# Sliding-window attention on one core: two half-empty key blocks as 32-query products, shared edge columns, a new order

## The chip, the cores and the metric

The kernel runs on one core of one Trainium2 chip. The metric is the device time of one execution in microseconds (us), the median of several runs. The engines of the core are TensorE (PE; its weight loads are listed as PEld), VectorE (DVE), ScalarE (ACT), GpSimd (POOL) and SyncE (SP), which issues most transfers. Each works through its own list of instructions in order and waits on semaphores for the others.

## What is computed

Four residual layers over a sequence of 2,048 positions with 512 features, in bf16: linear attention (A), sliding-window attention (B), A, B. Both have 32 heads of 16 features. The change lies in B:

```python
def _B_ref(x, wqkv, wo):
    B, S, D = x.shape
    H = 32; Dh = D // H; W = 256
    ...
    scores = jnp.einsum("bhqd,bhkd->bhqk", q, k) * (Dh ** -0.5)
    idx = jnp.arange(S)
    mask = (idx[:, None] - idx[None, :] >= 0) & (idx[:, None] - idx[None, :] < W)
    scores = jnp.where(mask[None, None], scores, -1e9)
    p = _softmax(scores, axis=-1)
    o = jnp.einsum("bhqk,bhkd->bhqd", p, v)
    return (lambda x, *d: x.transpose(*d))(o, 0, 2, 1, 3).reshape(B, S, D) @ wo

x = A_x
x = x + _A_ref(_layernorm(x, axis=-1), A_wqkv, A_wo)
x = x + _B_ref(_layernorm(x, axis=-1), B_wqkv, B_wo)
x = x + _A_ref(_layernorm(x, axis=-1), A_wqkv, A_wo)
x = x + _B_ref(_layernorm(x, axis=-1), B_wqkv, B_wo)
```

So a query sees itself and the 255 keys before it.

## The kernel before

**Stages.** `build` (L252) makes a graph of operations in this order: the keys of the first layer A (`layer_a_keys`), a `barrier` in which its sums over all positions are closed, `middle(2)`, a second `barrier`, and `middle(3)`. `middle(2)`, here phase 2, runs tile by tile over 16 tiles of 128 positions: the output of the first A, the first B, and already the keys and values of the second A. `middle(3)`, here phase 3, does the output of the second A, the second B and the stores. The queries of the second A stand between.

**Scores.** For a tile j of 128 keys, two blocks b of 64 keys are taken apart. Keys of two heads are interleaved on the 128 partitions (64 keys x 2 heads), so 16 head pairs are worked on (f = 0 to 3, gq = 0 to 3). `b_scores` (L617) multiplies each block with the 256 queries from its own first position on: eight products (L634) in 32x128 array tiles, into four PSUM banks; two exponentials on ScalarE (L644) write them as bf16 into a buffer P (`pb`, for every fourth tile of phase 3 a part of `vp`); a product with a triangle on DVE (L652) zeroes the first 64 columns above the diagonal. A key still reaches up to 255 positions on, so columns 256 to 319 of the block are made by `b_far` (L708): 32 products of 64 columns (L723), two exponentials (L732), and a mask (`far_masks`, L695) for each of the two blocks, either by GpSimd (L703) or by DVE (L704). In P, a block has 384 columns, of which the last 64 (and, for the next tile, the 64 ahead of the first) are zeros.

**Values.** `b_values` (L738) is called twice for each query tile j, for h = 0 and 1, with eight head pairs each. It sums over six key blocks; the part of P for the 128 queries is the stationary operand, the values with a column of ones (34 columns for two heads) the moving one (L753). Of the six blocks, block 2j-4 is the far end of the window, of which only the first 64 queries of the tile see anything; block 2j+1 is the second half of the tile's own keys, which only the last 64 queries see. For the other 64 queries both hold zeros. Then follow the reciprocal of the ones' column (L765) and a product (L766), a transpose by DMA, the output product (L400) and the residual sum (L568), and in phase 2 the normalisation (L361 to L365, two of its steps, L363 and L364, on GpSimd) and keys and values of the next A.

**Order.** `place` (L92) decodes the table at the end of the file: the place of every operation in one global order, the engine of each operation that may run on more than one (PSUM copies on ScalarE or DVE, far masks on DVE or GpSimd, stores issued by SP or GpSimd), and the PSUM bank of each tile. `synchronise` (L133) puts in the waits. The costs in the code (`mm`, `act`, `dve`, `par`) play no part once the table stands.

**Modes.** Three shapes of the array occur: full, 32x128 (scores; `spread`, L550), and 128x32 (denominators of A, `den`, L537: four tiles of 32 columns beside each other).

`b_edge` (L660) is there but not called: `PACK` (L218) is empty.

## Time and profile before

| what | us |
| --- | --- |
| median of 3 runs (416.87 to 417.95) | 416.91 |
| the profiled execution | 415.97 |
| its span, first to last instruction | 414.2 |
| PE busy, of the span | 387.9 (94%) |
| DVE busy | 346.8 (84%) |
| ACT busy | 345.8 (83%) |
| POOL busy | 117.7 (28%) |
| L644, exponentials of the scores, 224 into `pb` | 206.7 |
| L644, 32 into `vp` | 26.5 |
| L753, value products into `ps` from `pb`, 2,560 | 83.2 |
| L732, exponentials of the far scores into `pb`, 50 | 49.6 |
| L703, far masks on POOL, 26 into `pb` | 29.8 |

The chain that ended last, as the page sums it up, is made up of PE 48%, ACT 35%, DVE 9%, DMA 5%. The granted TensorE clock was 0.999 over the span. A busy share is an average: the last fourteen us hold little work on any engine, and the stages before are limited by different engines, so the stretches of the windows have to be read one by one. A line such as L400, L414 or L389 belongs to a helper (products of a tile with a weight, PSUM copies) that many operations share; the names of the tiles tell them apart. Durations of TensorE's products contain the time until the result stands, so starts, not durations, tell how closely products follow each other.

### The profile page before, as it was taken

What the parts mean: (1) busy time and instruction counts of PE and PEld (TensorE: products, weight loads), DVE (VectorE), ACT (ScalarE), POOL (GpSimd) and SP (SyncE); (2) the same over time, 40 slices, a digit from 0 to 9 for tenths busy, and PEclk for the clock granted to TensorE, in tenths of its full rate; (3) what the DMA queues carried; (4) which work ended last, traced back from release to release, by engine and by line L of the source; (5) the groups of instructions that cost most, each with busy time, mean ns of one, the idle gap of its engine ahead of it and who ended that gap; (6) DMA issues with size and microseconds to landing.
All of it is one profiled execution on the core that took longest, in us unless ns stands there. A gap on an engine that the chain in (4) does not pass through costs nothing.

```text
span 414.2 us, 17130 instructions
## 1 busy us (share of the span) xinstructions
PE 387.9 (94%) x7481; PEld 258.5 (62%) x7555; DVE 346.8 (84%) x803; ACT 345.8 (83%) x432; POOL 117.7 (28%) x211
## 2 busy tenths in 40 slices
PE   7999999999999999999999999999999989988886
PEld 3545676766575577565666777586757745556554
DVE  5997898989989988778978689989799687776575
ACT  2624449998999999999997245999999999999992
POOL 4784833111241243230112302220132215230111
PEclk9999999999999999999999999999999999999999
DMA  7545316632233624444213100353306623273361
GB/s 246 177 79 148 104 40 119 131 92 68 64 96 78 110 73 113 80 107 106 56 29 69 26 2 27 93 148 79 81 7 134 137 56 95 60 159 96 93 121 54
DMA packets 67555, 37.83 MB, mean 91 GB/s; under 512 B 48248, under 2 KB 62584, under 8 KB 67480
## 3 DMA queue, kind: packets, MB, share of 16 engines
q1 hardware_dynamic: 67040, 35.54, 36.7%
q8 instruction: 60, 0.98, 1.0%
q0 software_dynamic: 432, 1.18, 0.9%
q14 instruction: 15, 0.12, 0.1%
q10 hardware_dynamic: 8, 0.00, 0.0%
HBM read 6.29 MB, written 2.10 MB: 20 GB/s over the span
## 4 chain that ended last, share of the span: by engine, by line
PE 48%; ACT 35%; DVE 9%; DMA 5%; issue 2%; SPq 1%
ACT pb L644 22%; PE ps L400 17%; PE ps L414 13%; PE ps L753 7%; ACT pb L732 6%; ACT vp L644 5%; PE ps L634 5%; PE ps L475 2%; DMA XQ<-xn 2%; DVE stats L361 2%; DMA xres<-in_A_x_dram 2%; DVE xres L568 1%; DVE XQ L557 1%; PE ps L723 1%; ACT vp L732 1%
## 5 line engine op out<-in xcount | busy, mean ns | idle before, releaser
L644 ACT ACTIVATE pb<-ps 128x1024 bf16<-128x1024 f32 (+2 forms) x224 | 206.7, 1042 | 4.5 <-PE ps L634 3.7
L753 PEld LDWEIGHTS ps<-vB,pb 128*128 128x128 bf16 x2560 | 77.5, 96 | 11.7 <-issue 4.6
L753 PE MATMUL ps<-vB,pb 128*128 128x34 bf16 x2560 | 83.2, 177 | 1.1 <-ACT pb L644 0.6
L414 PE MATMUL ps<-xT,wBp 128*128 128x128 bf16 x1024 | 69.2, 219 | 1.2 <-DVE vp L586 0.5
L414 PEld LDWEIGHTS ps<-xT,wBp 128*128 128x128 bf16 x1024 | 59.2, 98 | 13.6 <-issue 4.4
L423 ACT ACTIVATE tE<-ps 128x512 bf16<-128x512 f32 x64 | 38.5, 612 | 34.3 <-PE ps L400 15.5
L363 POOL TENSOR_SCALAR ve<-mv 128x1 f32<-128x1 f32 x64 | 16.7, 261 | 172.6 <-DVE mv L362 170.5
L634 PE MATMUL ps<-XQ,kB 32*128 32x256 bf16 (+2 forms) x1024 | 49.6, 267 | 5.0 <-ACT vp L644 1.4
L732 ACT ACTIVATE pb<-ps 128x1024 bf16<-128x1024 f32 x50 | 49.6, 1066 | 0.4 <-PE ps L723 0.2
L568 DVE TENSOR_TENSOR xres<-ps,xres 128x512 bf16<-128x512 f32 x63 | 43.1, 685 | 7.6 <-PE ps L400 7.0
L400 PE MATMUL ps<-wA,XQ 128*128 128x512 bf16 x176 | 46.2, 379 | 2.7 <-issue 0.6
L652 DVE TENSOR_TENSOR pb<-pb,tri 128x512 bf16<-128x512 bf16 x112 | 44.7, 412 | 4.0 <-ACT pb L644 3.7
L703 POOL TENSOR_SCALAR_AFFINE_SELECT pb<-pb 128x1024 bf16<-128x1024 bf16 x26 | 29.8, 1148 | 62.9 <-DVE pb L652 32.6
L361 DVE BATCH_NORM_STATS2 stats<-xres 128x6 f32<-128x512 bf16 x64 | 43.6, 686 | 2.6 <-DMA xres<-in_A_x_dram 1.8
L364 POOL TENSOR_TENSOR rs<-ve,negh 128x1 f32<-128x1 f32 x64 | 37.8, 591 | 5.3
L634 PEld LDWEIGHTS ps<-XQ,kB 32*128 32x128 bf16 x1024 | 15.5, 92 | 33.6 <-ACT pb L644 9.2
L414 PE MATMUL ps<-XQ,wA 128*128 128x128 bf16 x512 | 34.7, 219 | 0.3 <-DVE o L766 0.3
L414 PEld LDWEIGHTS ps<-XQ,wA 128*128 128x128 bf16 x512 | 30.4, 98 | 5.7 <-DVE o L766 0.6
L400 PE MATMUL ps<-wBv,xT 128*128 128x512 bf16 x112 | 31.5, 380 | 2.2 <-issue 1.3
L400 PE MATMUL ps<-wBo,oT 128*128 128x512 bf16 x105 | 28.8, 380 | 4.2 <-issue 1.1
L400 PE MATMUL ps<-M,XQ 128*128 128x512 bf16 x112 | 30.7, 380 | 2.1 <-issue 1.0
L765 DVE RECIPROCAL rc<-ps 128x16 f32<-128x16 f32 x64 | 16.1, 252 | 19.3 <-PE ps L753 19.0
(110 smaller groups left out, 532.8 us busy)
## 6 DMA issues: line engine op xcount, KB each, us to landing
vB<-vS SPq DMA_DIRECT2D x64, 136.0 KB, 2.6
kB<-vp SPq DMA_DIRECT2D x64, 128.0 KB, 2.7
wA<-in_A_wqkv_dram SPq DMA_DIRECT2D x3, 512.0 KB, 4.6
out_dram<-xres POOLq DMA_DIRECT2D x9, 128.0 KB, 2.8
xres<-in_A_x_dram SPq DMA_DIRECT2D x2, 512.0 KB, 4.3
pb<-in_B_wqkv_dram SPq DMA_DIRECT2D x1, 1024.0 KB, 5.6
xres<-in_A_x_dram SPq DMA_DIRECT2D x3, 256.0 KB, 4.8
out_dram<-xres SPq DMA_DIRECT2D x6, 128.0 KB, 2.4
```

Source lines behind the costliest of these rows:

```text
L361: self.on("DVE", "stats", lambda e: e.bn_stats(K.stats[:, t, :], K.xres[:, t, :]), key, dve(512), rd=[("xres", t)], wr=[("stats", t)])
L364: self.pow = self.on("POOL", "pow", lambda e: e.tensor_tensor(K.rs[:, t, :], K.ve[:, t, :], K.negh[:], ALU.pow), key + 0.03, (640, 690), r ...
L400: m = e.matmul(K.ps(ps), lhs(c), rhs(c), start=c == 0, stop=c == 3)
L414: m = e.matmul(K.ps(ps)[:, f * P:(f + 1) * P], w(c, f), xT(c), start=c == 0, stop=c == 3)
L423: self.on("ACT", "E", lambda e: e.activation(K.tE[:, s, :], K.ps(ps), ACT.Exp, bias=0.0), key, act(512), wr=[("tE", s)], ps=[ps])
L568: self.on("DVE", "res", lambda e: e.tensor_tensor(K.xres[:, t, :], K.ps(po), K.xres[:, t, :], ALU.add), key, dve(512), rd=[("xres", t)], w ...
L634: m = e.matmul(K.ps(ps[gq])[:, ns * i:ns * i + ns], K.kB[rows, j % 4, 2 * f + b, :, :], K.XQ[rows, f, q:q + ns], start=True, stop=True, ti ...
L644: return e.activation(out(2 * h, 2, ns), i, ACT.Exp, bias=0.0, scale=0.25)
L652: return e.tensor_tensor(x, x, K.tri[:, 0, sh:64].unsqueeze(1).unsqueeze(1).to_broadcast([P, 4, n, 64 - sh]), ALU.mult)
L703: return e.affine_select(out=x, in_=x, compare_op=ALU.is_ge, fill=0.0, base=-2, pattern=[[0, 16], [-2, 64]], channel_multiplier=1)
L732: return e.activation(far(h), i, ACT.Exp, bias=0.0, scale=0.25)
L753: m = e.matmul(K.ps(ps)[:, 34 * u:34 * u + 34], K.P((b // 2) % rp)[:, gq, f, o:o + P], K.vB[:, (b // 2) % 4, b % 2, r, :], start=i == 0, s ...
```

## The change

In `b_values`, for the tiles listed in a new table `HALF` (phase 2: tiles 2 to 15; phase 3: tiles 2 to 8), the two half-empty blocks are taken out of the sum. A new operation `ph`, one for each h, adds them to the same PSUM bank afterwards: for each of the eight head pairs four products of 32 queries and 34 columns, in the array's 128x32 tiles; two take the far block's first 64 queries, two the own second block's last 64. The reads (and so the waits) of both operations are listed block by block.

`PACK` now names tile 9 of phase 3. There the scores of `b_scores` start 32 queries later, and `b_edge` makes columns 0 to 31 and 288 to 319 of each block in one go in place of `b_far`: keys 0 to 31 of a block against the first, keys 32 to 63 against the last, as products of 32 columns in 32x64 array tiles. One DVE product (`ma`) masks the first columns and copies them to their place.

The table of orders, engines and banks is another one. Beside what follows from the above it puts seven PSUM copies of phase 2 from ScalarE to DVE and one from DVE to ScalarE (three small ones around the barriers change sides too), eleven far masks from DVE to GpSimd, and two stores from GpSimd to SP.

```diff
-PACK = {}
+PACK = {3: [9]}
+HALF = {2: tuple(range(2, 16)), 3: tuple(range(2, 9))}
...
     def b_edge(self, j, key):
...
-                        c = 128 * f + 64 * b
-                        m = e.matmul(K.ps(ps[gq])[:, c:c + 64], K.kB[rows, j % 4, 2 * f + b, :, :], bass_view(K.XQ[rows, f, q:q + 32], [[288, 2], [1, 32]]), start=True, stop=True, tile_position=(32 * gq, 0))
+                        c = 64 * f + 32 * b
+                        for u in range(2):
+                            q = P * j + 64 * b + 288 * u
+                            half = slice(64 * u, 64 * u + 64)
+                            m = e.matmul(K.PS[half, ps[gq].banks[0], c:c + 32], K.kB[rows, j % 4, 2 * f + b, 32 * u:32 * u + 32, :], K.XQ[rows, f, q:q + 32], start=True, stop=True, tile_position=(32 * gq, 64 * u))
...
-            self.on("DVE", "gc", lambda e, side=side: e.tensor_copy(side(0), side(32)), key, dve(512), ps=two)
...
-                return e.activation(edge(h), K.pair(two, [[128, 4], [64, 2], [1, 32]]), ACT.Exp, bias=0.0, scale=0.25)
+                return e.activation(edge(h), K.pair(two, [[64, 4], [32, 2], [1, 32]]), ACT.Exp, bias=0.0, scale=0.25)
...
     def b_values(self, j, h, key):
...
-        blocks = [(2 * j, 0), (2 * j + 1, -64), (2 * j - 1, 64), (2 * j - 2, 128), (2 * j - 3, 192), (2 * j - 4, 256)]
+        blocks = [(2 * j, 0), (2 * j - 1, 64), (2 * j - 2, 128), (2 * j - 3, 192)]
+        ends = [(2 * j - 4, 256), (2 * j + 1, -64)]
+        apart = j in self.halves
+        if not apart:
+            blocks += ends
...
-                        m = e.matmul(K.ps(ps)[:, 34 * u:34 * u + 34], K.P((b // 2) % rp)[:, gq, f, o:o + P], K.vB[:, (b // 2) % 4, b % 2, r, :], start=i == 0, stop=i == len(blocks) - 1)
+                        m = e.matmul(K.ps(ps)[:, 34 * u:34 * u + 34], at(b, c, gq, f, P), val(b, 4 * f + gq), start=i == 0 and (not apart or u == 0), stop=not apart and i == len(blocks) - 1, skip_group_check=apart)
...
+        if apart:
+            def put(e):
+                m = None
+                for u in range(8):
+                    f, gq = 2 * h + u // 4, u % 4
+                    for g in range(4):
+                        b, c = ends[g // 2]
+                        m = e.matmul(K.ps(ps)[32 * g:32 * g + 32, 34 * u:34 * u + 34], at(b, c + 32 * g, gq, f, 32), val(b, 4 * f + gq), start=False, stop=True, tile_position=(0, 32 * g), skip_group_check=True)
+                return m
+            self.pe("ph", put, key + 0.01, 32, 34, mode=(128, 32), rd=reads((2 * h, 2 * h + 1), ends), ps=[ps])
```

## The prediction

> **What bounds the kernel now.** I read the windows first, cut at the places where the chain of waits changes its engine. Columns are the stretch, its length, and the busy time of TensorE (PE), weight loads, VectorE (DVE), ScalarE (ACT) and GpSimd (POOL).

> ```profile
> 115.00:170.00 55.00, 52.96 (x1176) 36.63 (x1191) 48.35 (x117) 54.88 (x64) 16.07 (x28) 1.00 0.45 92
> 170.00:205.00 35.00, 33.40 (x688) 21.21 (x683) 29.92 (x68) 34.22 (x41) 8.08 (x13) 1.00 0.35 87
> 205.00:278.00 73.00, 71.00 (x1236) 49.49 (x1249) 62.24 (x142) 52.26 (x77) 15.16 (x28) 1.00 0.23 56
> 278.00:322.00 44.00, 42.69 (x948) 29.66 (x953) 38.64 (x88) 43.28 (x51) 9.30 (x15) 1.00 0.35 79
> 322.00:400.00 78.00, 69.28 (x1667) 45.87 (x1675) 56.38 (x128) 77.29 (x86) 18.50 (x25) 1.00 0.44 100
> ```

> Phase 2 (first sliding-window layer, about 60 to 230 us) uses TensorE and ScalarE up together: 52.96 and 54.88 of 55 us. From 205 to 278 ScalarE has air (52.26 of 73) and TensorE none (71.00). From 278 to 400 it is ScalarE (120.6 of 122 us), with 8.7 us of air on TensorE after 322.

> Then the chain of waits, start and length in us; it names the engine that sets the time in each stretch:

> ```profile
> 161.13 9.20 ACT pb L644 x10
> 170.38 2.33 PE ps L400 x10
> ...
> 252.28 1.79 PE ps L414 x32
> ...
> 379.99 14.24 ACT pb L644 x16
> ```

> So TensorE work taken out of phase 2 is worth its length, ScalarE work taken out of phase 3 (second sliding-window layer, from about 260) too, and TensorE work taken out of phase 3 next to nothing.

> **What TensorE pays now.** Timeline of TensorE; a group's length is from its first start to the modelled end of its last product.

> ```profile
> 44.78 0.24 PE L537 MATMUL ps<-ones,eps 128*32 128x128 bf16 x4
> 44.85 0.40 PE L537 MATMUL ps<-XQ,zs 128*32 128x128 bf16 x16
> 45.18 0.62 PE L414 MATMUL ps<-XQ,wA 128*128 128x128 bf16 x8
> ...
> 86.64 0.41 PE L723 MATMUL ps<-XQ,kB 32*128 32x64 bf16 x32
> ...
> 187.95 0.40 PE L634 MATMUL ps<-XQ,kB 32*128 32x256 bf16 x8
> 188.28 1.37 PE L753 MATMUL ps<-vB,pb 128*128 128x34 bf16 x48
> 189.58 0.40 PE L634 MATMUL ps<-XQ,kB 32*128 32x256 bf16 x8
> ```

> A value product of 34 columns lasts 177 ns alone, so 48 of them start (1370-177)/47 = 25.4 ns apart; call it 25. The far scores, 32 products of 64 columns in four row tiles (188 ns alone), start (410-188)/31 = 7.2 ns apart, 29 ns for four. The denominators are the one operation in the new shape, 128x32: 16 products of 128 columns (219 ns alone) start (400-219)/15 = 12 ns apart on average, their groups of four 56 ns apart, as far as full products of 128 columns do.
> A change of array mode costs too. The last of the 48 value products starts at 188.28+1.37-0.177 = 189.47, the scores at 189.58: 110 ns instead of 25. The last denominator starts at 45.03, the next full product at 45.18: 150 ns instead of 56. About 85 to 95 ns for each change.

> **The change, part by part.**
> *Half blocks (phase 2, tiles 2 to 15; phase 3, tiles 2 to 8; two halves each, so 28 and 14 places).* Each place loses 2 blocks x 8 head pairs = 16 full products: 16 x 25 = 400 ns. It gains 32 products in 8 groups of four, and one stay in another mode. No row shows a group of four column tiles with 34 columns. Bounds: 25 ns a group (nothing in the trace starts its full products closer, and four at once at that pace would be free); 56 ns (the denominators, same shape, longer stream). I take 29, the far scores' group: four small products that do run side by side, nearest in columns. Between a last value product and the scores behind it, 7 x 29 + 110 = 313 ns come in for 400 out: 87 ns saved a place. With 25 it is 115 saved, with 56 and 150 at the exit it is 142 lost.
> [...]
> The order of both built programs counts the mode changes: 152 to 184 in phase 2, 157 to 172 in phase 3. The 28 places explain 28 of the 32 new ones; 4 more cost 4 x 95 ns = 0.4 us. Phase 2: 28 x 87 ns - 0.4 = **2.0 us** off TensorE (2.8 at 25 ns a group; 4.4 more at 56). It lies on the path from 170 to 278; up to 170, where the chain runs through ScalarE, it counts because the next item relieves ScalarE too. In phase 3 the 14 places save some 1.2 us, under the exponentials: 0 on the path. If they cost instead (2 us at 56 ns), the 8.7 us of air after 322 covers part.

> *Copies and masks moved.* In phase 2, ScalarE loses seven PSUM copies (three value, two next-layer value, one query, one transpose) and gains one: mean of such a copy 0.6 to 0.7 us, 0.49 in the chain, so 2.9 to 4 us, more than the 2.0 that TensorE loses. They land on DVE at 0.69 us. DVE gives back 11 far masks, 7 of them in phase 2 (L704, 682 ns, 7.5 us in all), to POOL, where one lasts 1,148 ns (L703). POOL has the time: 16.07 of 55 us busy. Cost 0, covered by POOL's idle time. Without cover, a mask that is late holds POOL's next eps and power (L363, L364: 261 + 591 ns), so the normalisation behind it, and the half blocks that read it.

> *One tile of shared edges (phase 3, tile 9).* Two exponentials of 1,024 columns (1,066 ns, L732) become two of 512 (594 ns, L644): 2 x 472 = 944 ns; the chain's pitch of an exponential, 9.20/10 = 920 ns, scaled by the columns gives 2 x 430. I take **0.9 us**, on the path (322 to 400). The 64 small score products replace 32: 230 ns become 230 (eight at once) to 460 ns, in TensorE's air. The added DVE product is one like L704 (0.69 us), DVE is busy 56 of 78 us there: 0.

> *Waits.* Full blocks no longer wait for the masks of the two end blocks; the new half-block step does, and behind it on TensorE stand scores in 20 of 42 places, which feed ScalarE. Value products (L753) waited for POOL's masks 0.3 us in all, so I take 0 for both. Summed with the prices above, the new order puts every score group of phases 2 and 3 as deep in TensorE's work as the old one, less the saving, to within 0.7 us: no stage is rebuilt.

> Sum: 2.0 + 0.9 = 2.9 us. The profiled execution took 415.97 us (span 414.2), so it would take 413.1; it lies 0.9 under the median of 416.91, from which I count: **414.0 us**.

> **Rivals.**
> A. *The TensorE time turns into waits.* For: up to 170 the chain is ScalarE's. Against: the same phase loses ScalarE copies. Only the edge's 0.9 us is left: 416.0, within 0.3% (1.25 us, about what a measurement of this kernel tells from no change).
> B. *A group of four is paced as the denominators are.* For: the same shape, and the only row of it. Against: full products of 128 columns also start 56 ns apart, so the stream explains it. Break-even is a group of 38 ns (7 G + 130 = 400). At 56: 416.9 + 28 x 0.142 + 0.4 - 0.9 = 420.4. Slower.
> C. *Far masks late on POOL.* For: POOL already stands 12.4 us in one wait before a mask. Against: value products waited 0.3 us in all for it. Each full mask on the path is 1.15 us, so the third one eats the gain; five of the eleven give 414.0 + 5.7 = 419.7. Slower.
> D. *The new order also finds waits.* TensorE stands idle 5.6 us from 115 to 278 (2.04 + 1.60 + 2.00); if 40% of that goes, 2.2 us more: 411.8.
> E. *Column tiles don't run side by side:* 32 x 25 = 800 ns a place, 28 x 0.5 = 14 us more: 430. The denominators (20 in under 0.5 us) speak against it.

> **How the numbers follow.** Forecast 0.50, D 0.16, A 0.13, B 0.10, C 0.09, E 0.02. Faster by over 0.3%: 0.50 + 0.16 = 0.66; within: 0.13; slower: 0.21. The range goes from a little under D, 410.8, to B's price, 420.2, leaving out part of B and C, E, and a still better order; for the forecast alone it is 412.5 to 415.5.

> **What would show it.** Products in 128*32 with 34 columns, 32 in a row: 0.38 us from first start to modelled end (7 x 29 + 177) if a group takes 29 ns, 0.57 at 56, 1.0 if one by one. Scores of phase 3 beginning some 2 us earlier than the 260 us of now; ScalarE's busy time in phase 2 down by 3 us and near 99% after 280; the exponentials of 512 columns at 594 ns. I am wrong if the groups take over 38 ns, if value products or normalisations wait for L703 by whole microseconds, or if ScalarE shows new gaps after 280.

## The result, and the profile after

| | us | ratio to before, 95% interval |
| --- | --- | --- |
| before, median of 20 runs (415.83 to 421.70) | 416.94 | |
| after, median of 20 runs (418.00 to 422.39) | 420.31 | 1.0078 [1.0062, 1.0095] |
| after, the profiled execution | 422.34 | |
| its span | 420.6 | |

The change makes the kernel 0.8% slower, 3.3 us; 2.9 us faster was forecast. The profiled execution is one of the longer ones, with a mean granted clock of 0.995. Eleven of the 20 runs of after show a clock of 0.995 or 0.996 and take 418.4 to 422.4 us; the nine at 0.998 or above take 418.0 to 420.3. Ratios here and below are estimates with their intervals, not quotients of the medians beside them, and leave out runs over 1.5% above the fastest of their kernel: below, that is two of the six of old_32 (426.87 and 427.51 us).

The windows of after, with the same cuts and columns as those of before (two stretches left out); the last three columns are the granted clock, the DMA share and GB/s:

```profile
115.00:170.00 55.00, 49.28 (x1212) 32.85 (x1223) 44.46 (x106) 50.31 (x58) 17.13 (x27) 0.97 0.43 85
...
205.00:278.00 73.00, 70.34 (x1380) 49.18 (x1395) 62.99 (x144) 51.48 (x76) 18.19 (x30) 1.00 0.22 51
...
322.00:400.00 78.00, 68.44 (x1794) 45.90 (x1804) 55.51 (x128) 76.00 (x85) 20.20 (x26) 1.00 0.40 92
```

The stretch that TensorE and ScalarE filled together, 115 to 170, now has air on both: TensorE 49.28 of 55 us (52.96 before), ScalarE 50.31 (54.88). Both were waiting for something else, and the clock dipped to 0.97. After 322 ScalarE has 2.00 us of air where it had 0.71.

The chain of waits says for what. Start and length in us; "issue" is time in which the engine waited for nothing that the profile shows:

```profile
116.55 0.65 PE ps L769 x22
117.20 1.27 issue
118.47 0.40 PE ps L769 x10
...
139.47 4.23 DMA XQ<-xn
143.80 0.41 DVE xn L366
144.24 2.71 DMA XQ<-xn
...
153.61 0.26 PE ps L779 x24
153.87 0.49 issue
154.36 0.23 PE ps L779 x8
...
328.43 1.25 issue
...
411.42 3.78 DMA oT<-o
```

Two new things stand in it. TensorE stops in the middle of a group of products whose operands are all there: after 22 of 32 value products (L769) at 117.20, after 24 of 32 half-block products (L779) at 153.87, after 20 of 32 far scores at 328.43. Before has no such stop. And the chain runs through transposes: of the normalised tile at 139.47 and 144.24, and of the last output tile at 411.42, where the same step of before took 2.40 us. VectorE's own row shows what the transpose at 139.47 held up:

```profile
143.80 0.41 DVE L366 TENSOR_SCALAR xn<-xres,mv,rs 128x512 bf16<-128x512 bf16 x1 [1.63 <-DMA XQ<-xn]
```

The timeline of TensorE, the rows that answer to the half blocks' price and to the first stop:

```profile
116.48 0.72 PE L769 MATMUL ps<-vB,pb 128*128 128x34 bf16 x22
118.47 0.40 PE L769 MATMUL ps<-vB,pb 128*128 128x34 bf16 x10 [1.27 <-issue]
118.80 0.38 PE L779 MATMUL ps<-vB,pb 128*32 128x34 bf16 x32
119.11 0.40 PE L635 MATMUL ps<-XQ,kB 32*128 32x256 bf16 x8
119.44 1.78 PE L415 MATMUL ps<-xT,wBp 128*128 128x128 bf16 x16
...
125.47 0.96 PE L769 MATMUL ps<-vB,pb 128*128 128x34 bf16 x32
126.36 0.38 PE L779 MATMUL ps<-vB,pb 128*32 128x34 bf16 x32
126.67 0.40 PE L635 MATMUL ps<-XQ,kB 32*128 32x256 bf16 x8
```

32 half-block products take 0.38 us, as forecast for groups 29 ns apart. Spread evenly that is (380-179)/31 x 4 = 26 ns for a group of four; the single starts in the trace have the second group 39 ns behind the first and the later ones mostly 25 ns apart, the pace of full products. From the first value product to the scores it is 126.67-125.47 = 1.20 us, where 48 full products took 189.58-188.28 = 1.30: 100 ns saved a place, 87 forecast.

**Where the time went.** I paired the groups of scores of both traces, operation by operation, and took the start in after less the start in before; this difference is called the shift. It compares one execution of each kernel, and that of after is a long one: the spans differ by 6.3 us (420.57 and 414.25), the medians by 3.4. So the table shows where time is lost, and overstates how much for a usual run. The shift changes at few places:

| at (us of before) | shift goes from, to | what stands there in after |
| --- | --- | --- |
| 118 to 124 | -0.2 to +2.3 | stop of 1.27 us, then the clock |
| 137 to 147 | 2.3 to 4.0 | wait for the transposes of the normalised tile |
| 147 to 166 | 4.0 to 4.5 | stop of 0.49 us |
| 166 to 262 | 4.5 to 4.5 (4.3 to 5.1 between) | no lasting loss, and no gain either |
| 262 to 281 | 4.5 to 5.0 | wait for a transpose |
| 323.6 to 325.4 | 4.5 to 5.95 | stop of 1.25 us |
| 341 to 366 | 5.96 to 5.33 | the shared edges gain |
| 405 to the end | 5.3 to 6.3 | last transpose, 3.78 us for 2.40 |

From 166 to 262 thirteen half-block steps save 100 ns each on TensorE, and the shift is 4.5 at both ends: none of it arrives.

### The profile page after: what moved, and what is told of

It is laid out like the page before. It is cut to its first block, busy times and chain, and to the rows that moved or that the text cites. A ratio compares the mean times of both kernels' runs of the same rounds, so it can differ in the third digit from the quotient of the medians.

```text
span 420.6 us, 18546 instructions
## 1 busy us (share of the span) xinstructions
PE 387.4 (92%) x8187; PEld 256.2 (61%) x8259; DVE 345.1 (82%) x800; ACT 342.3 (81%) x425; POOL 128.4 (31%) x220
## 4 chain that ended last, share of the span: by engine, by line
PE 43%; ACT 30%; DVE 16%; DMA 7%; issue 3%; SPq 0%; POOL 0%; DVEq 0%
ACT pb L645 18%; PE ps L401 14%; PE ps L415 9%; PE ps L769 6%; ACT pb L733 5%; PE ps L635 5%; ACT vp L645 4%; DMA xT<-xn 3%; DVE XQ L558 2%; DVE stats L362 2%; DMA XQ<-vp 2%; PE ps L779 2%; DMA XQ<-xn 2%; DVE xres L569 1%; PE ps L476 1%
## 5 line engine op out<-in xcount | busy, mean ns | idle before, releaser
L415 PE MATMUL ps<-xT,wBp 128*128 128x128 bf16 x1024 | 69.9, 221 | 1.8 <-DMA xT<-xn 1.5
L704 POOL TENSOR_SCALAR_AFFINE_SELECT pb<-pb 128x1024 bf16<-128x1024 bf16 x36 | 41.2, 1145 | 91.6 <-DVE pb L653 48.9
L769 PEld LDWEIGHTS ps<-vB,pb 128*128 128x128 bf16 x1936 | 61.5, 96 | 11.7 <-issue 4.0
L769 PE MATMUL ps<-vB,pb 128*128 128x34 bf16 x1936 | 66.5, 177 | 1.8 <-issue 1.3
L415 PEld LDWEIGHTS ps<-xT,wBp 128*128 128x128 bf16 x1024 | 59.3, 98 | 13.3 <-issue 5.1
L364 POOL TENSOR_SCALAR ve<-mv 128x1 f32<-128x1 f32 x64 | 17.0, 266 | 151.4 <-DVE mv L363 149.4
L401 PE MATMUL ps<-wA,XQ 128*128 128x512 bf16 x177 | 47.3, 384 | 4.7 <-issue 1.2
L733 ACT ACTIVATE pb<-ps 128x1024 bf16<-128x1024 f32 x48 | 47.5, 1066 | 0.7 <-PE ps L724 0.6
L653 DVE TENSOR_TENSOR pb<-pb,tri 128x512 bf16<-128x512 bf16 (+1 forms) x112 | 45.1, 415 | 3.1 <-ACT pb L645 3.0
L365 POOL TENSOR_TENSOR rs<-ve,negh 128x1 f32<-128x1 f32 x64 | 37.0, 577 | 5.3
L415 PE MATMUL ps<-XQ,wA 128*128 128x128 bf16 x512 | 35.2, 219 | 0.0
L415 PEld LDWEIGHTS ps<-XQ,wA 128*128 128x128 bf16 x512 | 30.7, 98 | 6.3 <-ACT pb L645 0.9
L401 PEld LDWEIGHTS ps<-wA,XQ 128*128 128x128 bf16 x192 | 16.2, 98 | 21.7 <-issue 2.2
```

Of the source, the lines that this page charges most:

```text
L365: self.pow = self.on("POOL", "pow", lambda e: e.tensor_tensor(K.rs[:, t, :], K.ve[:, t, :], K.negh[:], ALU.pow), key + 0.03, (640, 690), r ...
L401: m = e.matmul(K.ps(ps), lhs(c), rhs(c), start=c == 0, stop=c == 3)
L415: m = e.matmul(K.ps(ps)[:, f * P:(f + 1) * P], w(c, f), xT(c), start=c == 0, stop=c == 3)
L653: return e.tensor_tensor(x, x, K.tri[:, 0, sh:64].unsqueeze(1).unsqueeze(1).to_broadcast([P, 4, n, 64 - sh]), ALU.mult)
L704: return e.affine_select(out=x, in_=x, compare_op=ALU.is_ge, fill=0.0, base=-2, pattern=[[0, 16], [-2, 64]], channel_multiplier=1)
L733: return e.activation(far(h), i, ACT.Exp, bias=0.0, scale=0.25)
```

## The experiments

Two families of kernels: "new" has the change's order, "old" the order, engines and banks of before with the half step put right behind the second value operation. Each kernel was timed beside runs of before on its own chip; the ratio is to those.

**1. Order against half step.** Four kernels: the change with the half step as 16 full products (new_full) and as 16 products of 64 queries in 128x64 tiles (new_64); the old order with 32-query (old_32) and 64-query (old_64) steps, without the shared edges.

```diff
-                    for g in range(4):
-                        b, c = ends[g // 2]
-                        m = e.matmul(K.ps(ps)[32 * g:32 * g + 32, ...], at(b, c + 32 * g, gq, f, 32), ..., tile_position=(0, 32 * g), ...)
+                    for g in range(2):
+                        b, c = ends[g]
+                        m = e.matmul(K.ps(ps)[64 * g:64 * g + 64, ...], at(b, c + 64 * g, gq, f, 64), ..., tile_position=(0, 64 * g), ...)
```

> The changed kernel with its own order, engines and waits; only the half-block step uses 16 full products (128 queries, 34 columns) instead of 32 of 32 queries. Theory S (instruction supply: the 64 densely packed instructions of a half-block step run TensorE's instruction stream dry, seen as three gaps of 1.45, 0.67 and 1.44 us inside a group of products, and a clock dip behind the first): no gap over 0.3 us inside a group, about 417 to 418 us although TensorE gets some 3.5 us more work. Theory O (the new order by itself costs the time, S is a side issue): 420 to 423 us.

> As before it, but the half-block step as 16 products of 64 queries in 128x64 tiles: eight groups of two, half the instructions for the same eight groups. S: no gaps inside a group, 416 to 417.5 us. O: 419 to 421 us. If two column tiles of 64 don't run side by side the step takes 16 x 25 = 400 ns instead of about 200 and the time is that of the full products.

> The order, engines and banks of the kernel before; only the half blocks are taken apart as in the change (32-query products, the step set right behind the second value product of its half); no shared edges. O: faster than before, 414 to 415.5 us, since TensorE loses some 2 us in phase 2. S: gaps inside groups again, 417 to 420 us. Third theory A (ScalarE and the waits between engines set the time in phase 2, TensorE's saving is worth nothing): within 1 us of before, no gaps.

> The kernel before with its order; half blocks as 64-query products in 128x64 tiles. S and O both: 414 to 415.5 us. A: within 1 us of before. S fails if gaps over 0.3 us inside a group show here as often as with 32 queries.

| | us | ratio, 95% | stops inside groups of products, us from start to start |
| --- | --- | --- | --- |
| new_full | 420.55 | 1.0088 [1.0065, 1.0111] | 0.35, 0.40, both after 400 |
| new_64 | 418.99 | 1.0059 [1.0041, 1.0076] | 0.38, 0.38, both after 399 |
| old_32 | 421.4 (all six: 423.17) | 1.0128 [1.0095, 1.0160] | 0.95, 1.11 |
| old_64 | 417.13 | 1.0012 [0.9999, 1.0026] | none |

Timeline of TensorE in old_32:

```profile
116.49 0.79 PE L769 MATMUL ps<-vB,pb 128*128 128x34 bf16 x25
118.06 0.34 PE L769 MATMUL ps<-vB,pb 128*128 128x34 bf16 x7 [0.77 <-issue]
```

and the same place in old_64:

```profile
116.91 0.97 PE L769 MATMUL ps<-vB,pb 128*128 128x34 bf16 x32
117.80 0.43 PE L779 MATMUL ps<-vB,pb 128*64 128x34 bf16 x16
118.16 0.40 PE L635 MATMUL ps<-XQ,kB 32*128 32x256 bf16 x8
```

(A gap of 0.60 us in old_32, at 277, isn't counted: the profile puts it down to a copy on VectorE, L587.) In after and these four, stops of over half a microsecond come with the 32-query step, in either order, and go without it, so the long ones are the step's (new_64_slots, below, has one of 0.65 us at 399). Halving the instructions of the step is worth 1.2% in the old order. Not all of that is the stops themselves: in the profile of old_32 the shift grows by 0.8 and 1.2 us at its two stops, by 1.2 at 160 and 0.8 at 277 where TensorE waits for a transpose and for that copy, and by 2.8 behind the last scores, where the last transpose takes 4.48 us (2.70 in old_64) and the clock falls to half. The new order costs 0.6 to 0.9% without the long stops, so it has a loss of its own: the times of new_full and new_64 lie in the ranges of theory O and above those of S. For old_64 both theories had 414 to 415.5 us; only A, within 1 us of before, holds. And old_64 saves TensorE 50 ns a place (118.16-116.91 = 1.25 us for 1.30), 1.4 us in phase 2's 28 places, and is no faster than before; the shift of its scores goes from 0.34 us at 62 to 0.15 at 222 and 0.69 at 397.

**2. Is TensorE's time worth anything there?** old_none: the old order, and no end blocks at all in those tiles.

The edit, seen from old_32:

```diff
-            self.pe("ph", put, key + 0.01, 32, 34, mode=(128, 32), ...)
```

> The order, engines and banks of before; the two end blocks of tiles 2 to 15 (phase 2) and 2 to 8 (phase 3) are left out of the value sums altogether, so 42 x 16 x 25 ns = 16.8 us of TensorE work (11.2 in phase 2, 5.6 in phase 3) is not done, and nothing is put in its place. Theory A (with the order of before, ScalarE and waits set the time where the products were; TensorE's time there is worth little): 412 to 416.5 us, not more than a third of the 11.2 us. Theory P (my prediction: TensorE's time in phase 2 is worth its length from 170 us on, and half of it before): 405 to 409 us.

421.17 us, 1.0079 [1.0047, 1.0111], above the ranges of both theories: 42 places x 0.4 us = 16.8 us of TensorE's work are gone, and the kernel is not faster. The timeline of TensorE shows where the time goes:

```profile
82.60 0.40 PE L635 MATMUL ps<-XQ,kB 32*128 32x256 bf16 x8 [1.75 <-DMA kB<-vp]
...
189.84 0.96 PE L769 MATMUL ps<-vB,pb 128*128 128x34 bf16 x32
191.09 0.40 PE L635 MATMUL ps<-XQ,kB 32*128 32x256 bf16 x8 [0.28 <-ACT pb L645]
191.55 0.97 PE L769 MATMUL ps<-vB,pb 128*128 128x34 bf16 x32
192.70 0.40 PE L635 MATMUL ps<-XQ,kB 32*128 32x256 bf16 x8 [0.19 <-ACT pb L645]
```

What the value products leave, the scores behind them wait for: their PSUM banks are still being read by ScalarE's exponentials, for 0.28 and 0.19 us in these rows. Over the whole execution scores wait 10.6 us for exponentials, where they waited 3.4 in before. The saving turns into a wait on the spot. From 170 to 224 us ten places lose 4.0 us of work, and the shift falls by 0.4. That the kernel is even slower comes from two jumps of the shift, 1.8 us at 75 to 80 and 1.5 at 158 to 166: behind the first stands a transfer of keys that took 4.47 us from its issue at 77.88 (2.14 for the same transfer in before), behind the second waits for a transpose and for another such transfer. Without them it would still stand some 0.8 us behind before (an estimate from the shifts: 4.1 at the end less 1.8 and 1.5), so they do not hide a gain of the size that was expected.

The opposite, dense: before with each far score product cut in two, 64 products of 32 columns for 32 of 64. No value product changes; the instructions double.

```diff
-                        m = e.matmul(K.ps(ps[gq])[:, c:c + 64], ..., K.XQ[rows, f, q:q + 64], ...)
+                        for u in range(2):
+                            d = c + 32 * u
+                            m = e.matmul(K.ps(ps[gq])[:, d:d + 32], ..., K.XQ[rows, f, q + 32 * u:q + 32 * u + 32], ...)
```

> The kernel before, without any column tile or new order: each far-score step makes its 64 columns by two products of 32 columns, 64 products (128 instructions) instead of 32, same weights, same result. Theory S (dense instruction streams run TensorE dry) without the change's own means: gaps of 0.5 to 1.5 us inside groups of products, 418 to 423 us. Rival N (the gaps belong to column tiles): no gap inside a group; the 28 x 0.17 us = 4.7 us more TensorE time then tells alone, and is worth little if theory A holds: 416.5 to 418 us.

429.24 us, 1.0253 [1.0219, 1.0287]. Timeline of TensorE in dense:

```profile
151.70 0.46 PE L725 MATMUL ps<-XQ,kB 32*128 32x32 bf16 x36
152.47 0.37 PE L725 MATMUL ps<-XQ,kB 32*128 32x32 bf16 x28 [0.31 <-issue]
...
405.84 0.20 PE L755 MATMUL ps<-vB,pb 128*128 128x34 bf16 x2
407.06 0.21 PE L755 MATMUL ps<-vB,pb 128*128 128x34 bf16 x1 [1.01 <-issue]
...
410.31 0.69 PE L725 MATMUL ps<-XQ,kB 32*128 32x32 bf16 x64
```

The same stops by another route: no column tiles, no new order, only more instructions in little time. Besides, a far step lasts 0.69 us for 0.41, and most of the 28 add those 0.28 us to the shift (28 x 0.28 = 7.8 us): TensorE's time ahead of scores counts in full here, and ScalarE waits for these: its exponentials stand 8.7 us in all for scores and 4.6 for far scores, where it was 3.7 and 0.2 in before. Behind them, under the exponentials, it counted for next to nothing in old_none. The time is above the 418 to 423 us of theory S, and not all of it is the far steps: of the 13.3 us of shift at the last scores, 2.6 come in one place at 134, where TensorE stands idle for 2.04 us behind VectorE's L365, and 1.5 at the stop of 1.01 us, each with half a clock for 3.4 us around it.

**3. What the new order lost.** new_64_slots gives the normalised tile of the next A a second buffer, in idle space of `pqd`; new_64_slots_pow also moves three operations of tile 4 around 266 us (the last lines, the order on three engines). old_64_slots is the control, new_32_slots_pow has the change's own step. The lines behind the last `...` put the packed table into words.

```diff
-                self.norm(j, k, 3, ...
+                self.norm(j, k, 3 + j % 2, ...
...
-POOL: eps 4, eps 5, power 5, power 4
+POOL: eps 4, power 4, eps 5, power 5
-DVE: vS copy 2, xn 4
+DVE: xn 4, vS copy 2
-SP: vB 5, kB 4, transpose 4
+SP: transpose 4, vB 5, kB 4
```

> The changed kernel with 64-query products; the normalised tile for the next A layer alternates between two buffers (the second is the space of a matrix that is idle in this phase), so that VectorE no longer waits there for the transpose of the tile before (1.63 us at 143.8 us in the changed kernel). Theory O1 (the +1.7 us between 137 and 147 us that all kernels with the new order show is this wait): ratio to before 0.3 to 0.5% lower than that of the 64-query kernel (1.0059), the step gone from the score groups' times. Rival O2 (the transposes are late for all, in SyncE's queue): the step stays, the ratio too.

> The same two buffers with the order of before and 64-query products (1.0012). O1: within 0.2% of that, since the order of before hardly waits there (0.6 us in all); a gain of 0.3% or more would make it faster than both kernels.

> As new_64_slots (the new order, half step as 16 products of 64 queries, a second buffer for the normalised tile), and around 266 us, in tile 4 of phase 3, three operations stand earlier in the order: GpSimd's power of tile 4 ahead of tile 5's variance step, VectorE's normalised tile ahead of a copy, and its DMA transpose ahead of two stores in SyncE's queue. Theory (the new order's last own wait is the one for this transpose, 1.37 us on TensorE at 272.7, behind it ScalarE 0.91): the transpose is issued at about 268 and not 269.85, the step of score times between 270 and 280 goes from +2.1 to under +0.8 us, and the time is some 1.2 us under new_64_slots, 0.998 of before. Rival (the step is the order's work in front of these scores, not the wait): the wait goes and the step stays, the time as new_64_slots, 1.0013.

> The same order and buffer with the change's own half step, 32 products of 32 queries. Theory (two separate losses, gaps inside dense stretches and the new order's two waits for the normalisation): both waits gone as in new_64_slots_pow, gaps of 0.6 to 1.5 us inside groups of products still there, 1.002 to 1.005 of before, above new_64_slots_pow by 0.002 to 0.006. Rival (the gaps are harmless, the waits were all of the loss): level with new_64_slots_pow within 0.002.

| | us | before, same chip | ratio, 95% |
| --- | --- | --- | --- |
| new_64_slots | 419.15 | 418.03 | 1.0013 [0.9990, 1.0037] |
| old_64_slots | 417.91 | 418.03 | 1.0007 [0.9977, 1.0037] |
| new_64_slots_pow | 417.93 | 416.86 | 1.0028 [1.0009, 1.0047] |
| new_32_slots_pow | 420.50 | 416.86 | 1.0065 [1.0044, 1.0086] |

The second buffer takes away the step of the shift between 137 and 147 (1.8 us in new_64, 0.0 here), and the ratio falls from 1.0059 to 1.0013 with intervals that do not overlap, though on different chips. It is the wait of 1.63 us shown for after: the program lets VectorE (L366) write over the tile only when the transpose that reads it, 4.23 us from 139.47 on, is done. Timeline of TensorE in new_64_slots, the next wait:

```profile
272.34 0.40 PE L635 MATMUL ps<-XQ,kB 32*128 32x256 bf16 x8
274.11 1.07 PE L415 MATMUL ps<-xT,wBp 128*128 128x128 bf16 x16 [1.37 <-DMA xT<-xn]
```

In new_64_slots_pow the transpose is issued at 267.43 instead of 269.85, and the wait is gone:

```profile
271.69 0.40 PE L635 MATMUL ps<-XQ,kB 32*128 32x256 bf16 x8
272.02 1.07 PE L415 MATMUL ps<-xT,wBp 128*128 128x128 bf16 x16
```

The step there falls from +2.1 to +0.7 us, as expected. The time in ratio does not: the two intervals overlap, and 0.998 is missed. In this profile nearly all scores from 300 to 397 us stand ahead of before's, by up to 1.24 us, and the end comes 1.4 us later: the chain waits 3.20 us at 398.95 and 4.27 us at 406.01 for transposes of the last output tiles. The tail is the loss that is left in this profile. It is not shown to be the order's: the last transpose took 2.43 and 2.45 us in new_64 and new_full, of the same order, and 4.48 in old_32, of the old one. No run changed it. Nor is the tail idle, short as its work is: in the last 14.2 us of before TensorE is busy for 9.66 us and VectorE for 8.53.

new_32_slots_pow, the same order with the change's own step, takes 2.6 us more on the same chip by the medians (ratios 1.0065 to 1.0028, whose intervals overlap by a hair), with stops of 0.89 and 1.36 us, start to start, where the 64-query step had one of 0.39 us. Its nine runs fall into two groups: four with a mean clock of 0.999 or 1.0 take 418.55 to 418.94 us, some 0.9 more than the 64-query kernel, and five with 0.995 or 0.996 take 420.50 to 421.34, some 3. Of the 64-query kernel's twelve runs one has such a clock. So the two losses are separate, and much of the stops' price is the dip of the clock that follows some of them.

**4. The parts of the table.** Engines exchanged (new_64_oldeng: new order, old engines; old_64_neweng the other way), and in the old order only phase 2's copies moved (old_64_copies: ten from ScalarE to DVE, four back) or only the far masks (old_64_masks: 19 from DVE to GpSimd, 8 back, eleven on balance). Only the engine entries of the table differ, in words for example

```diff
-copy of values, phase 2: ACT
+copy of values, phase 2: DVE
```

> The changed kernel with 64-query products (419.0 us), its order and banks, but every operation that may run on two engines on the engine it had before: far masks, PSUM copies, stores. Theory E (the moved masks and copies cost the time): back to 417 us. Theory O (the sequence and the banks cost it): 418.5 to 421 us.

> The counterpart: order and banks of before with 64-query products (417.1 us), and the engines of the changed kernel. E: 418.5 to 420 us. O: within 1 us of 417.1; if ScalarE's relief of some 3 us in phase 2 is worth what I predicted, 414 to 416.

> Order and banks of before, 64-query products (1.0012 of before), and of the changed kernel's engine moves only the PSUM copies of phase 2 (ten from ScalarE to VectorE, four back). If ScalarE sets the time of phase 2, its 3 to 4 us less are worth 2 to 3 us: 0.994 to 0.997 of before. If VectorE's later copies hold up what follows in an order made for the old engines: 1.004 or more.

> The same kernel with only the far masks moved as in the changed kernel (19 from VectorE to GpSimd, 8 back). If late masks on GpSimd are the price of the moved engines (all moves together: 1.0131 of before): 1.006 to 1.012. If it is the copies: within 0.2% of 1.0012.

Expected were 417 or 418.5 to 421 us for new_64_oldeng and up to 420 for old_64_neweng; both came out longer. new_64_oldeng took 428.42 us, 1.0243 [1.0205, 1.0281]; old_64_neweng 423.58, 1.0131 [1.0083, 1.0178]; old_64_copies 420.18, 1.0068 [1.0044, 1.0091]; old_64_masks 420.40, 1.0077 [1.0048, 1.0106]. Exchanging the engines costs in both orders, so order and engines are made for each other. In old_64_copies ScalarE loses work and scores come 2.4 us later at 147 and 4.8 at 333. Moving work off the engine that the page calls full gave nothing without a new order.

**5. The shared edges.** new_64_nopack is new_64 without them; old_pack9 is before with tile 9 only, old_pack4 with tiles 9, 11, 12 and 13, the edges placed ahead of the tile's scores.

```diff
-PACK = {3: [9]}
+PACK = {3: [9, 11, 12, 13]}
```

> The changed kernel with 64-query products, but tile 9 of phase 3 with its far scores again, made at the place where the shared edges stood. If the edges save 0.9 us as predicted: 419.9 us. If the small products and the added waits cost it: 418 us or less.

> The kernel before with full products everywhere and its order; only tile 9 of phase 3 makes its edges in one tile (64 products of 32 columns, two exponentials of 512 columns) ahead of its scores, which move on by one place each. If ScalarE's 0.9 us is worth its length from 322 us on: 0.9978 of before (416.0 for 416.9). If the rotated places cost it: 1.000 or more.

> The same for tiles 9, 11, 12 and 13: 4 x 0.9 = 3.6 us less on ScalarE. If it holds, 0.991 to 0.993 of before, faster than both kernels; if VectorE's added products or the dense 64-product steps take it back, 0.997 or more, with gaps inside groups.

new_64_nopack took 421.94 us, 1.0085 [1.0058, 1.0112], so the edges are worth 0.0026 x 417 = 1.1 us in the new order by the middle values; the intervals overlap and the chips differ. old_pack9 is slower than before, 1.0042 [1.0013, 1.0071]: the shift is +1.0 at 345, +4.6 at 351.6 behind the early edges and +2.6 from 366 on. old_pack4 is at +18 us at 403, 1.0375 [1.0328, 1.0421]; part of that is the clock, at half speed for 13.65 us from 409.55 of its own time and for 3.4 us twice before. Early edges push the tile's own scores back.

**6. How far a profile repeats.** before_again is the kernel of before once more.

> The kernel before, unchanged, for a trace on the same chip: the spread of the score groups' times between two profiles of one kernel. If steps of a microsecond show here too, steps of that size in one profile of another kernel prove nothing by themselves.

417.29 us, 1.0001 [0.9966, 1.0036]. Its scores differ from those of the first profile by 0.9 to 1.2 us (1.4 in one place), an offset from the start without a step of a microsecond. So steps of that size in the tables above are not the usual difference of two profiles of one kernel. Two of its eight runs have a mean clock of 0.996 and take 421.3 us: a dip of the clock came to the kernel of before as well, in two runs of eight for eleven of the 20 of after.

No kernel beat before. old_64, old_64_slots and new_64_slots are level with it.

## Why the prediction was wrong

**Half blocks, 2.0 us: the price right, its worth wrong.** The group takes 26 ns on average for 29, the place saves 100 ns for 87. The step that failed reads "TensorE work taken out of phase 2 is worth its length", and for this term "it lies on the path from 170 to 278". It came from busy shares and a chain with both engines in it. old_none shows that 16.8 us less of value products bring no gain in the old order: the scores behind them wait for ScalarE, 10.6 us for 3.4. In after itself, thirteen steps that save 100 ns each leave the shift where it was. dense shows that the same engine's time ahead of the scores counts in full there, 0.28 us at most of 28 places. Rival A had the mechanism, but nothing on the losing side: it gave 416.0.

**What was missing: instructions.** 64 instructions for the step (32 products, 32 weight loads) in 0.3 us in place of 32 in 0.4 was not a term at all. The stops take 1.27 + 0.49 + 1.25 = 3.0 us of TensorE in the profile of after, and the dip of the clock behind the first some 1.2 us more (2.5 of shift less 1.27). old_32 against old_64 (1.0128 to 1.0012) and the pair of part 3 show the stops to be the step's. How the 3.4 us between the medians divide among stops, dips and waits isn't shown: these sizes are those of one long execution.

**Waits, 0: wrong.** "No stage is rebuilt" was taken from the depth of TensorE's work ahead of each score group. That says nothing about where on DVE, GpSimd and SyncE's queue the normalised tile stands. The tile's buffer cost 1.7 us, shown by taking it away, in the trace and in the time. One late transpose cost 1.4 us of the step at 270 to 280, shown in the trace; the time did not fall with it. The tail's 1.0 us stays open, as its transpose is as short as before's in other kernels of the new order.

**Copies and masks, 0.** Neither's price can be taken by itself: in the old order each adds 0.6 to 0.7% to old_64, in the new one both are part of it. Rival C, masks late on GpSimd, isn't seen in after: value products idle 0.3 us for ScalarE's exponentials and none for L704.

**Shared edges, 0.9 us: about right in size**, -0.6 us in the shift of after, 1.1 by ratios whose intervals overlap, and exponentials of 512 columns at 594 ns as forecast. In the old order (old_pack9) the gain isn't there.

**Rivals B, D and E.** B and E fall with the 26 ns. That B's price, 420.4 us, and C's, 419.7, stand next to the measured 420.31 is luck: neither cause is in the trace. D, that the new order fills some of the old one's waits, had the wrong sign: it adds its own.

## What to carry to other kernels

Before work is taken off an engine that is 94% busy, as TensorE was in before, look at what stands right behind that work and what it waits for. Here 0.28 us more of work ahead of the scores, which feed the other full engine, counted in full at most of 28 places (dense), and 16.8 us less of work that lay under that engine's time gave no gain (old_none). Cutting a product into smaller tiles was paid in instructions as well as in time: 64 far scores of 32 columns for 32 of 64 took 0.69 us for 0.41, and dense shows stops of 0.31 and 1.01 us. So watch the count per microsecond: 64 queries for 32 halved it in the step and, in the old order, removed the loss (1.0012 for 1.0128). A moved or re-ordered step has to be followed on every queue that serves it, down to the buffer that its transpose still reads, which cost 1.7 us here.

## What the runs showed of the hardware

**The clock fell to half behind a stop of 1.27 us in after and around one of 1.01 us in dense.** Windows of after behind the first stop; the third number from the end is the granted clock:

```profile
118.00:120.00 2.00, 1.53 (x57) 1.25 (x57) 1.14 (x3) 0.99 (x2) 0.00 (x0) 0.90 0.57 171
120.00:122.00 2.00, 1.78 (x14) 1.45 (x13) 0.75 (x3) 1.50 (x2) 0.00 (x0) 0.50 0.34 73
122.00:124.00 2.00, 2.00 (x25) 0.92 (x24) 1.15 (x6) 1.04 (x2) 1.09 (x3) 0.75 0.62 130
```

and of dense around its stop of 1.01 us:

```profile
406.00:408.00 2.00, 0.99 (x29) 0.86 (x27) 0.60 (x3) 1.44 (x2) 0.00 (x0) 0.70 0.56 116
408.00:410.00 2.00, 1.55 (x26) 0.91 (x27) 1.01 (x3) 1.20 (x2) 0.00 (x0) 0.50 0.45 101
```

In after (0.10 + 0.50 + 0.25) x 2 us = 1.7 us of full clock are lost, which is 3.4 us at half speed. The 16 products of L415 take 1.78 us there and 1.07 elsewhere. Not every stop did it: the one of 1.25 us at 328.43 left the clock at 1.00. A dip came without such a stop too: dense has one at 137.13, around the wait of 2.04 us that ends at 137.63, and it came and went between runs of one kernel (clock 0.995 or 0.996 in eleven of the 20 of after). It was more frequent with the 32-query step in the two pairs run side by side: four of six runs of old_32 and none of twelve of old_64 have a mean clock under 0.997, five of nine of new_32_slots_pow and one of twelve of new_64_slots_pow. Four of twelve runs of old_64_slots, without that step, have it too.

**Two tiles of 64 columns took 34 ns, four of 32 columns 26.** 16 products in 128x64 tiles take 0.43 us, (430-177)/15 x 2 = 34 ns for a group of two; four in 128x32 take 26 ns, a full product 25. All three are averages over a step; why the two wide tiles started less closely isn't known from these runs.
